# One core, a gated mix of an H3 convolution and dilated local attention: the kernel written anew with an explicit issue order

## The chip, the core and the metric

The program runs on one core of a Trainium2 chip. The core has five engines, each with its own stream of instructions: TensorE (PE: matmuls from SBUF into PSUM; a matmul loads its stationary operand first, shown as PEld), VectorE (DVE), ScalarE (ACT), GpSimd (POOL) and SyncE (SP, which here only issues DMAs; POOL issues others). The metric is the device time of one execution in microseconds, lower is better. The median of three runs of the kernel before is 402.83 us (400.19 to 403.54).

## What is computed

```python
def _A_ref(q, k, v, shift_k, ssm_k, ssm_D):          # S = 2048, D = 640, 4 taps
    k_shift = sum of k shifted by 0..3 rows, times shift_k
    kv = k_shift * v
    y = causal convolution of kv with ssm_k along S  # rfft of length 4096, product, irfft
    return q * (y + kv * ssm_D)
def _B_ref(x, wqkv, wo):                             # 32 heads of 20; window of 8 keys, step 2
    q, k, v = split(x @ wqkv)
    logits = q . k[pos - 2*w], w = 0..7, masked where pos - 2*w < 0
    return (softmax(logits) @ v[pos - 2*w]) @ wo
x = A_q
g = sigmoid((x * gate_w).sum(-1))
return g * a + (1 - g) * b                           # a = _A_ref(x, ...), b = _B_ref(x, ...)
```

(shortened to the formulas). All tensors are 2,048 x 640 in bf16, wqkv is 640 x 1,920.

## The kernel before

Three functions run one after the other; the order of instructions inside them is chosen by the framework's planner, which ranks ready instructions by priority and estimated cost. Only the matmuls of the transform are held in program order by a token (L191).

*b_proj* (L330) loads x, transposes it with PE into xT, and computes q and k feature-major (L376: 128 features x 512 positions from five matmuls, copied to stg by ACT, L379). Each head's 20 features are then moved by SP's DMAs from stg into q32 and k32, where a head begins on a multiple of 32 partitions (L388). The values are projected in 18 blocks of 114 positions (L404, L406), with a column of ones per head in VW that later gives the softmax sum. Beside it, DVE forms kv (*a_kv*, L93): four quarters, each with four products and three additions of 2,560 elements per partition (L131 to L134) and a product with v that also reorders (L135). POOL's queue loads k and v for it (L116, L121, L124).

*b_attn* (L409) walks over block groups outside and eight groups of four heads inside: 40 steps of up to four blocks. A step has scores for two pairs of heads (L454), exp by ACT (L460), a product with the band mask by DVE (L461), PV matmuls with the masked exps as stationary operand (L476), a reciprocal and a product by DVE (L481, L485). After eight steps the group's output is transposed (L495), multiplied with wo (L423), scaled with 1 - g (L426) and written to the DRAM scratch b_scr by SP.

*a_fft* (L149) computes the convolution as a transform of 32 x 64 points in two steps, for four groups of 20 channels in each of eight slots. Per group: first step for the filter (h) and for kv (u) (s1, L206, evacuated to Am by ACT, L196); second step in 64-row halves of the array (s2, L224, L226), evacuated for h by DVE together with the addition of D (L244), for u by ACT (L261); a copy of Hs with its halves swapped (L247, L248); two products (L263, L264); the inverse's first step (L278, evacuated to Cm by ACT) and its second (L298 on), whose result DVE multiplies with g * A_q (L307) and POOL, in the last group DVE, adds b to (L308). The output leaves with the last group (L315). The tables Gre, Gim, Hre, Him, A_q and b_scr are loaded at the start of this function (L167 to L183), into memory that attention has used.

## Time and profile before

| | |
|---|---|
| median of three runs | 402.83 us (400.19 to 403.54) |
| span of the profiled execution, first to last instruction | 400.5 us |
| busy: PE, PEld, DVE, ACT, POOL | 274.8, 183.9, 229.0, 194.6, 91.8 us |
| DMA | 37.37 MB in 26,552 packets, mean 93 GB/s |
| granted TensorE clock, mean over the span | 0.777 |

The profile gives no other time for that execution than its span, which lies inside the range of the runs. A row of a group of instructions reads: line, engine, operation, output and input tile, shape, count, then busy time and the mean of one instruction in ns, then the time its engine idled before them and what ended that idle time. Busy PE time is modelled, since matmuls overlap in the array; a PE that is busy need not be at its peak.

### The profile page before, as it was taken

What the parts mean: (1) busy time and instruction counts of PE and PEld (TensorE: products, weight loads), DVE (VectorE), ACT (ScalarE), POOL (GpSimd) and SP (SyncE); (2) the same over time, 40 slices, a digit from 0 to 9 for tenths busy, and PEclk for the clock granted to TensorE, in tenths of its full rate; (3) what the DMA queues carried; (4) which work ended last, traced back from release to release, by engine and by line L of the source; (5) the groups of instructions that cost most, each with busy time, mean ns of one, the idle gap of its engine ahead of it and who ended that gap; (6) DMA issues with size and microseconds to landing.
All of it is one profiled execution on the core that took longest, in us unless ns stands there. A gap on an engine that the chain in (4) does not pass through costs nothing. (4 is left out here: it accounts for less than half of the span.)

```text
span 400.5 us, 9049 instructions
## 1 busy us (share of the span) xinstructions
PE 274.8 (69%) x3958; PEld 183.9 (46%) x3958; DVE 229.0 (57%) x294; ACT 194.6 (49%) x302; POOL 91.8 (23%) x97
## 2 busy tenths in 40 slices
PE   0699999875543697978878676861766784787640
PEld 0465555332222465555545345641653573476630
DVE  0331094999698867666685307649753538083540
ACT  1025545422543758585875282860446391936310
POOL 5029502090005300000000061000046008102840
PEclk9999999989655568685859596785696697769695
DMA  8926997575334901010101079999000000000047
GB/s 235 283 75 108 163 183 172 111 156 63 68 112 90 173 19 36 18 52 2 51 2 50 34 259 275 231 291 138 0 3 2 2 2 2 2 2 4 2 95 169
DMA packets 26552, 37.37 MB, mean 93 GB/s; under 512 B 15616, under 2 KB 21364, under 8 KB 26000
## 3 DMA queue, kind: packets, MB, share of 16 engines
q1 hardware_dynamic: 21136, 19.62, 20.8%
q0 software_dynamic: 5232, 17.13, 19.7%
q8 instruction: 31, 0.51, 0.6%
q14 instruction: 9, 0.07, 0.1%
q10 hardware_dynamic: 144, 0.04, 0.0%
HBM read 26.26 MB, written 5.25 MB: 79 GB/s over the span
## 5 line engine op out<-in xcount | busy, mean ns | idle before, releaser
L460 ACT ACTIVATE ET<-sc 128x912 bf16<-128x912 f32 (+1 forms) x80 | 63.9, 855 | 21.2 <-PE O L476 11.0
L376 PE MATMUL pj<-xT,W 128*128 128x512 bf16 x200 | 49.9, 405 | 10.0 <-ACT stg L379 10.0
L308 POOL TENSOR_TENSOR a_lin<-a_lin,b_lin 128x480 bf16<-128x480 bf16 (+1 forms) x18 | 32.8, 1856 | 104.1 <-DVE a_lin L307 104.1
L461 DVE TENSOR_TENSOR ET<-ET,band 128x912 bf16<-128x912 bf16 (+1 forms) x80 | 45.4, 570 | 14.5 <-ACT ET L460 13.3
L190 PE MATMUL pb<-Am,Gre 64*128 64x80 bf16 x512 | 32.4, 233 | 27.4 <-DVE Hs L244 14.7
L196 ACT CAST Am<-pa 128x512 bf16<-128x512 f32 x80 | 41.2, 725 | 17.4 <-PE pa L190 17.4
L454 PE MATMUL sc<-q,k 20*128 20x114 bf16 x576 | 32.0, 257 | 18.8 <-ACT ET L460 17.7
L190 PEld LDWEIGHTS <-Gim 64*128 64x128 bf16 x512 | 27.9, 119 | 31.7 <-issue 31.7
L196 ACT CAST Cm<-pa 128x512 bf16<-128x512 f32 x40 | 21.0, 612 | 42.7 <-PE pa L190 42.7
L244 DVE TENSOR_TENSOR Hs<-pb,Dg 128x960 bf16<-128x960 f32 (+1 forms) x24 | 23.9, 1041 | 29.5 <-PE pb L190 29.4
L379 ACT CAST stg<-pj 128x512 bf16<-128x512 f32 x40 | 22.6, 589 | 30.8 <-PE pj L376 20.1
L376 PEld LDWEIGHTS <-W 128*128 128x128 bf16 x200 | 20.3, 103 | 35.5 <-issue 16.0
L423 PE MATMUL op<-wo,oT 128*128 128x512 bf16 (+1 forms) x160 | 33.1, 362 | 3.4 <-ACT fin L426 3.4
L190 PE MATMUL pb<-Am,Gim 64*128 64x80 bf16 x512 | 33.1, 235 | 0.0
L476 PE MATMUL O<-VW,ET 128*128 128x21 bf16 x576 | 22.4, 179 | 13.1 <-DVE o_S L485 12.8
L406 ACT CAST VW<-psv 128x640 bf16<-128x640 f32 x18 | 12.6, 700 | 36.5 <-PE psv L404 36.5
L307 DVE TENSOR_TENSOR a_lin<-pa,a_lin 128x480 bf16<-128x480 f32 (+1 forms) x24 | 13.3, 591 | 28.9 <-PE pa L190 28.9
L190 PEld LDWEIGHTS <-Gre 64*128 64x128 bf16 x512 | 28.7, 119 | 1.1 <-issue 0.8
L476 PEld LDWEIGHTS <-ET 128*128 128x128 bf16 x576 | 19.3, 102 | 18.3 <-issue 12.7
L454 PEld LDWEIGHTS <-k 20*128 20x128 bf16 x576 | 16.7, 107 | 23.2 <-issue 17.9
L190 PE MATMUL pa<-MU,Up 128*128 128x128 bf16 x160 | 24.0, 252 | 3.3 <-DVE a_lin L307 3.3
L426 ACT ACTIVATE fin<-op,omg 128x640 bf16<-128x640 f32 x16 | 12.7, 794 | 27.7 <-PE op L423 19.7
(76 smaller groups left out, 502.8 us busy)
## 6 DMA issues: line engine op xcount, KB each, us to landing
h_lin<-in_A_v_dram POOLq DMA_DIRECT2D x4, 640.0 KB, 16.2
h_lin<-in_A_ssm_k_dram POOLq DMA_DIRECT2D x8, 320.0 KB, 6.7
b_scr<-fin SPq DMA_DIRECT2D x16, 160.0 KB
W<-in_B_wqkv_dram SPq DMA_DIRECT2D x3, 800.0 KB
kh<-in_A_k_dram POOLq DMA_DIRECT2D x12, 190.0 KB, 13.1
q<-stg SPq DMA_DIRECT2D x28, 80.0 KB
k<-stg SPq DMA_DIRECT2D x28, 80.0 KB
Him<-ca_Him POOLq DMA_DIRECT2D x1, 2048.0 KB, 17.7
```

The lines of the kernel that those rows point to most:

```text
L190: inst = nc.tensor.matmul(*args, **kwargs)
L196: nc.scalar.copy(dst, src)
L244: nc.vector.tensor_tensor(Hs[:, :, :, j0:j0 + nj, :], view, Dgv.unsqueeze(3).to_broadcast([128, 2, IL, nj, 4]), ALU.add)
L307: nc.vector.tensor_tensor(reg, yv, reg, ALU.mult)
L308: (nc.vector if g == NG - 1 else nc.gpsimd).tensor_tensor(reg, reg, breg, ALU.add)
L376: nc.tensor.matmul(ps[:], lhsT=W[:, dt, which, 128 * ft:128 * ft + 128], rhs=xT[:, dt, HALO + 512 * sc:HALO + 512 * sc + 512], start=(dt = ...
L379: nc.scalar.copy(stg[:, 512 * sc:512 * sc + 512], ps[:])
L423: nc.tensor.matmul(op[:, n0:n1], lhsT=oT[:, ft, HALO + 128 * sb:HALO + 128 * sb + 128], rhs=wo[:, ft, n0:n1], start=(ft == 0), stop=(ft == ...
L454: nc.tensor.matmul(sc[:, hh, bb * BP:bb * BP + BP], lhsT=k32[32 * h4:32 * h4 + DH, t, kc:kc + 128], rhs=q32[32 * h4:32 * h4 + DH, t, qc:qc ...
L460: nc.scalar.activation(dst, src, ACT.Exp, scale=SCALE)
L461: nc.vector.tensor_tensor(dst, dst, band[:].unsqueeze(1).unsqueeze(1).to_broadcast([128, 2, nbb, BP]), ALU.mult)
L476: nc.tensor.matmul(O[:, slot * 21:slot * 21 + 21], lhsT=ET[:, h4, bb, :], rhs=VW[:, b, h, :], start=True, stop=True, skip_group_check=True)
```

## The change

Everything between the constants and the launch is rewritten. The planner is switched off (`tc.manual_schedule()`): every engine and every queue takes its instructions in the order of the program text, and pieces of work are interleaved by Python generators.

- Positions are split into even and odd ones, so that the window of 8 keys with step 2 becomes 8 neighbours; 17 blocks of 121 queries replace 18 of 114.
- kv is formed in 24 pieces between the value projections, in half quarters; loads of k and v go through SP.
- The band mask leaves DVE: 11 constant rows beside the 20 features of each head in k and q (mk, mq) add 0 inside the window and a large negative number outside, inside the score matmul.
- Attention walks over head groups outside and block groups inside, in 80 half steps. The projection of q and k for the first 256 features (20 of 50 chunks) stands before it, the other 30 chunks stand between half steps 10 and 50. Three buffers of k and q each hold one head group.
- g * A_q is computed early and kept in the DRAM scratch qg_scr. The output projection moves behind attention and runs between the steps of the transform; POOL's queue writes b_scr.
- The transform has five groups of 16 channels per slot; the first step also uses the array's halves, evacuations are 1,024 elements wide and are shared by ACT and DVE by an estimate in the text; the swap Hw is two DMAs, D is added to the filter's first point; the inverse's second step runs once, behind everything, for all channels (160 columns), and the output leaves from there.

The core of the new text (the replaced functions are shown above; memory set-up and constants are cut):

```diff
+BP = 121
+NB = 17
+PRE = 7
+HS = 1024 + PRE
+XW = 2072
+NF = 11
+NT = 8
+KW = 128 * NB
+QW = BP * NB
+GROUPS = [[0, 1, 2, 3], [4, 5, 6, 7], [8, 9, 10], [11, 12, 13], [14, 15, 16]]
...
+NG = 5
+IL = 16
...
+    def pick(self, n):
+        ca, cd = n * 0.833 + 80, n * 1.042 + 70
+        if self.t["a"] + ca <= self.t["d"] + cd:
+            self.t["a"] += ca
+            return "a"
+        self.t["d"] += cd
+        return "d"
...
+    kv = p0.tile([128, 2, 64, 80], BF, name="kv", tag="kv")
+    vl = p0.tile([128, 64, 160], BF, name="vl", tag="hl")
+    xS = p0.tile([128, 16, D], BF, name="xS", tag="oS")
...
+    load_x(0); load_w(2); load_x(1)
...
+    load_kv(0)
+    load_x(2); load_x(3); load_w(0); load_w(1)
+    load_kv(1)
...
+        for h4 in range(4):
+            nc.sync.dma_start(ksets[e][32 * h4 + DH:32 * h4 + DH + NF, :], ca["mk"].ap())
+            nc.sync.dma_start(qsets[e][32 * h4 + DH:32 * h4 + DH + NF, :], ca["mq"].ap())
...
+    def kv_gen():
...
+        for c in range(4):
+            kh = khs[c]
+            for hf in range(2):
+                n0 = 8 * hf
+                pr = p1.tile([128, 4, 8, 160], BF, name="pr", tag="pr")
+                for j in range(4):
+                    nc.vector.tensor_tensor(pr[:, j], kh[:, n0 + 3 - j:n0 + 11 - j, :],
+                                            wl[:, j, :].unsqueeze(1).to_broadcast([128, 8, 160]), ALU.mult)
+                    if j % 2 == 1:
+                        yield
+                nc.vector.tensor_tensor(pr[:, 0:2], pr[:, 0:2], pr[:, 2:4], ALU.add)
+                nc.vector.tensor_tensor(pr[:, 0], pr[:, 0], pr[:, 1], ALU.add)
+                n = 16 * c + n0
+                nc.vector.tensor_tensor(kv[:, :, n:n + 8, :].rearrange("p c n i -> p n c i"),
+                                        pr[:, 0].rearrange("p n (c i) -> p n c i", c=2),
+                                        vl[:, n:n + 8, :].rearrange("p n (c i) -> p n c i", c=2), ALU.mult)
+                yield
+            if c < 2:
+                load_kv(c + 2)
...
+    kvg = kv_gen()
...
+    def qk_gen(engs):
+        for ft in range(NDT):
+            for which in range(2):
+                stg = p1.tile([128, KW], BF, name="stg", tag="stg", bufs=2)
...
+                        yield
+                f0 = 128 * ft
+                for h in range(f0 // DH, (f0 + 127) // DH + 1):
+                    fa, fb = max(DH * h, f0), min(DH * h + DH, f0 + 128)
+                    r = 32 * (h % 4) + fa - DH * h
+                    dst = (qsets if which == 0 else ksets)[(h // 4) % 3]
+                    w = QW if which == 0 else KW
+                    frag = (dst[r:r + fb - fa, 0:w], stg[fa - f0:fb - f0, 0:w])
+                    if h // 4 - 3 < done_t[0]:
+                        nc.sync.dma_start(*frag)
+                    else:
+                        pending.append((h // 4, frag))
...
+    for c in range(3):
+        transposes(c)
+        for b in range(4 * c, 4 * c + 4):
+            vproj(b)
+            advance(kvg, 1)
+    transposes(3)
+    gate()
+    for sb in range(16):
+        nc.vector.tensor_scalar(xS[:, sb, :], xS[:, sb, :], g_sb[:, sb:sb + 1], None, ALU.mult)
+    for c in range(4):
+        nc.sync.dma_start(qg_scr.rearrange("(t p two) d -> p two t d", p=128, two=2)[:, c // 2, 4 * (c % 2):4 * (c % 2) + 4, :],
+                            xS[:, 4 * c:4 * c + 4, :])
...
+    def scores_done(t):
+        done_t[0] = t + 1
+        for fr in [p for p in pending if p[0] - 3 == t]:
+            nc.sync.dma_start(*fr[1])
...
+    qk = qk_gen(lambda ft, w, c: "a" if ft < 2 else "d")
+    advance(qk, 10)
+    advance(kvg, 4)
+    for b in range(12, NB):
+        vproj(b)
+        advance(kvg, 1)
+    advance(qk, 10)
...
+    def scores(s):
+        t, gi, hf = halves[s]
+        blocks = GROUPS[gi]
+        nw = BP * len(blocks)
+        kb, qb = ksets[t % 3], qsets[t % 3]
+        sc = ppa.tile([128, 2, 512], F32, name="sc", tag="sc")
+        for bb, b in enumerate(blocks):
+            for hh in range(2):
+                r = 32 * (2 * hf + hh)
+                nc.tensor.matmul(sc[:, hh, BP * bb:BP * bb + BP], lhsT=kb[r:r + DH + NF, 128 * b:128 * b + 128],
+                                 rhs=qb[r:r + DH + NF, BP * b:BP * b + BP], start=True, stop=True,
+                                 tile_position=(r, 0), skip_group_check=True)
+        nc.scalar.activation(ETs[s % NET][:, :, 0:nw], sc[:, :, 0:nw], ACT.Exp, scale=SCALE)
...
+    scores(0)
+    for s in range(len(halves)):
+        if s + 1 < len(halves):
+            scores(s + 1)
+            if s + 1 == len(halves) - 1 or halves[s + 2][0] != halves[s + 1][0]:
+                scores_done(halves[s + 1][0])
+        if 10 <= s < 20 or 21 <= s < 31 or 41 <= s < 51:
+            advance(qk, 1)
+        advance(kvg, 1)
+        pv(s)
...
+    for q in range(4):
+        for c in range(2):
+            base = A_ssm_k[160 * q + 80 * c:160 * q + 80 * c + 80, :]
+            src = bass.AP(tensor=base.tensor, offset=base.offset, ap=[[64, 32], [S, 80], [1, 64]])
+            nc.sync.dma_start(h_lin[32 * q:32 * q + 32, :, c, :], src)
...
+    p2 = ctx.enter_context(tc.tile_pool(name="p2", bufs=1, reuse_waits="tile"))
...
+    G = p2.tile([128, 32, 2, 128], BF, name="G")
+    nc.sync.dma_start(G[:], cf["G"].ap().rearrange("p (a r b) -> p a r b", a=32, r=2))
...
+    def op_gen():
+        for b in range(NB):
+            tr = pp2.tile([128, NDT, 128], BF, name="tr", tag="ps")
+            for ft in range(NDT):
+                nc.tensor.transpose(tr[:, ft, 0:BP], oS[0:BP, b, 128 * ft:128 * ft + 128], ident[0:BP, 0:BP])
+            oT = oTs[b % 3]
+            ld.copy(oT[:, :, 0:BP], tr[:, :, 0:BP], 605)
+            yield
...
+            if ld.pick(640) == "a":
+                nc.scalar.activation(fin[0:BP, :], opf[0:BP, 0:D], ACT.Copy, scale=omg[0:BP, b:b + 1])
+            else:
+                nc.vector.tensor_scalar(fin[0:BP, :], opf[0:BP, 0:D], omg[0:BP, b:b + 1], None, ALU.mult)
+            for r0, n, dst in pos_rows(b_scr, BP * b, BP):
+                nc.gpsimd.dma_start(dst, fin[r0:r0 + n, :])
+            yield
...
+    def s1_gen(key, X, g):
+        Am = p2.tile([128, 64, 4, IL], BF, name="Am", tag="Am", bufs=3)
+        st[key] = Am
+        for oc in range(2):
...
+            for il in range(8):
+                i = IL * g + 8 * oc + il
+                for qp in range(2):
+                    rows = slice(64 * qp, 64 * qp + 64)
+                    if key[0] == "h":
+                        lhsT = X[rows, i, :, :].rearrange("p c n -> p (c n)")
+                    else:
+                        lhsT = X[rows, :, :, i].rearrange("p c n -> p (c n)")
+                    o = pss[qp][:, il // 4, 128 * (il % 4):128 * (il % 4) + 128]
+                    nc.tensor.matmul(o, lhsT=lhsT, rhs=F1b[rows, :], start=True, stop=True,
+                                     tile_position=(64 * qp, 0), skip_group_check=True)
+            for qp in range(2):
+                src = pss[qp][:].rearrange("p a (l q j) -> p j q (a l)", l=4, q=2)
+                ld.copy(Am[:, :, 2 * qp:2 * qp + 2, 8 * oc:8 * oc + 8], src, 1024)
...
+    def s2_gen(key, dst):
+        Am = st.pop(key)
+        for jb in range(4):
+            ps = ps_tile("s2")
+            for jj in range(8):
+                j = 8 * jb + jj
+                for r in range(2):
+                    for c in range(2):
+                        rows = slice(64 * c, 64 * c + 64)
+                        nc.tensor.matmul(ps[:, c, 64 * jj:64 * jj + 64], lhsT=G[rows, j, r, :],
+                                         rhs=Am[rows, 2 * j + r, :, :].rearrange("p q l -> p (q l)"),
+                                         start=(r == 0), stop=(r == 1), tile_position=(64 * c, 0), skip_group_check=True)
+            ld.copy(dst[:, :, 8 * jb:8 * jb + 8, :, :].rearrange("p c j q l -> p c (j q l)"), ps[:], 1024)
...
+    def h_s2(g):
+        Hs = p2.tile([128, 2, 32, 4, IL], BF, name="Hs", tag="Hs", bufs=2)
+        yield from s2_gen(("h", g), Hs)
+        Hw = p2.tile([128, 2, 32, 4, IL], BF, name="Hw", tag="Hw")
+        nc.sync.dma_start(Hw[0:64], Hs[64:128])
+        nc.sync.dma_start(Hw[64:128], Hs[0:64])
...
+    def u_s2(g):
+        Up = p2.tile([128, 2, 32, 4, IL], BF, name="Up", tag="Up", bufs=2)
+        yield from s2_gen(("u", g), Up)
+        Hs, Hw = st.pop(("H", g))
+        Vp = p2.tile([128, 2, 32, 4, IL], BF, name="Vp", tag="Vp")
+        for c in range(2):
+            nc.vector.tensor_tensor(Vp[:, c], Up[:, c], Hw[:, c], ALU.mult)
+            nc.vector.tensor_tensor(Up[:, c], Up[:, c], Hs[:, c], ALU.mult)
+        ld.t["d"] += 4500
+        st[("UV", g)] = (Up, Vp)
...
+    def inv1(g):
+        Up, Vp = st.pop(("UV", g))
...
+                ps = ps_tile("i1")
+                for il in range(8):
+                    o = ps[:, il // 4, 128 * (il % 4):128 * (il % 4) + 128]
+                    for k, src in ((0, Up), (1, Vp)):
+                        nc.tensor.matmul(o, lhsT=src[:, c, :, :, 8 * oc + il].rearrange("p j q -> p (j q)"), rhs=M[:, k, :],
+                                         start=(k == 0), stop=(k == 1), skip_group_check=True)
+                i0 = IL * g + 8 * oc
+                ld.copy(Cm[:, :, :, c, i0:i0 + 8].rearrange("p n r l -> p (n r) l"),
+                        ps[:].rearrange("p a (l m) -> p m (a l)", l=4), 1024)
...
+    def fft_gen():
+        yield from s1_gen(("h", 0), h_lin, 0)
+        yield from h_s2(0)
+        yield from s1_gen(("u", 0), kv, 0)
+        for g in range(NG):
+            if g + 1 < NG:
+                yield from s1_gen(("h", g + 1), h_lin, g + 1)
+            yield from u_s2(g)
+            if g + 1 < NG:
+                yield from h_s2(g + 1)
+                yield from s1_gen(("u", g + 1), kv, g + 1)
+            yield from inv1(g)
+    fft = fft_gen(); opg = op_gen()
+    k = 0
+    while advance(fft, 1):
+        k += 1
+        if k >= 2:
+            advance(opg, 1)
+    while advance(opg, 1):
+        pass
...
+    qg = p0.tile([128, 64, 160], BF, name="qg", tag="hl")
+    bl = p0.tile([128, 64, 160], BF, name="bl", tag="kv")
+    tabs = []
+    for k in range(4):
+        tb = p2.tile([128, 2, 16, 128], BF, name="tab", tag="Am" if k < 3 else "Hw", bufs=3 if k < 3 else 1)
+        nc.sync.dma_start(tb[:], cf["T"].ap()[:, 4096 * k:4096 * k + 4096].rearrange("p (r a b) -> p r a b", r=2, a=16))
+        tabs.append(tb)
+    for q in range(4):
+        nc.sync.dma_start(qg[32 * q:32 * q + 32], lin_src(qg_scr, q, 0, 64))
+    for q in range(4):
+        nc.gpsimd.dma_start(bl[32 * q:32 * q + 32], lin_src(b_scr, q, 0, 64))
+    for n0 in range(0, 64, 6):
...
+        ps = ps_tile("i2")
+        for k in range(nn):
+            n2 = n0 + k
+            o = ps[:, k // 3, 160 * (k % 3):160 * (k % 3) + 160]
+            for r in range(2):
+                nc.tensor.matmul(o, lhsT=tabs[n2 // 16][:, r, n2 % 16, :], rhs=Cm[:, n2, r, :, :].rearrange("p c i -> p (c i)"),
+                                 start=(r == 0), stop=(r == 1), skip_group_check=True)
+        for hb in range(0, nn, 3):
+            m = min(3, nn - hb)
+            reg = qg[:, n0 + hb:n0 + hb + m, :]
+            yv = ps[:, hb // 3, 0:160 * m].rearrange("p (n c) -> p n c", n=m)
+            nc.vector.tensor_tensor(reg, yv, reg, ALU.mult)
+        reg = qg[:, n0:n0 + nn, :]
+        nc.vector.tensor_tensor(reg, reg, bl[:, n0:n0 + nn, :], ALU.add)
+        for q in range(4):
+            dst = outf[:, 160 * q:160 * q + 160].rearrange("(a b) c -> a b c", b=64)[:, n0:n0 + nn, :]
+            (nc.sync, nc.gpsimd)[q % 2].dma_start(dst, reg[32 * q:32 * q + 32])
```

722 lines of the change are left out of this document (261 added, 461 removed).

## The prediction

> **What bounds the kernel now.** The chain of waits ends after a few links (its shares add up to a few per cent), so it names no bound. I cut the span at the places where the kind of work changes and read the busy time in each stretch.
>
> ```profile
> core 0: us, PE busy (x) PEld busy (x) DVE busy (x) ACT busy (x) POOL busy (x), PEclk, DMA share, GB/s
> 0.00:13.00 13.00, 0.88 (x8) 0.72 (x9) 0.00 (x0) 1.28 (x1) 5.64 (x13) 1.00 0.86 267
> 13.00:108.00 95.00, 81.47 (x551) 41.92 (x550) 58.22 (x38) 36.97 (x61) 31.71 (x41) 0.95 0.68 132
> 108.00:235.00 127.00, 91.00 (x1400) 59.03 (x1400) 85.75 (x184) 77.45 (x102) 12.27 (x13) 0.66 0.23 57
> 235.00:283.00 48.00, 27.09 (x443) 19.39 (x442) 30.71 (x16) 23.29 (x43) 4.70 (x6) 0.68 0.98 236
> 283.00:388.00 105.00, 74.35 (x1560) 62.88 (x1559) 54.29 (x57) 55.59 (x98) 35.09 (x22) 0.80 0.03 6
> 388.00:400.50 12.50, 0.00 (x0) 0.00 (x0) 0.00 (x0) 0.00 (x0) 2.37 (x4) 0.55 0.79 177
> ```
>
> Loading takes 13 us. The projections (95 us) are held by PE. Attention with its output projection (127 us) fills no engine: PE 72%, DVE 68%, ACT 61%. The first 48 us of the transform run at the rate of the DMA (share 0.98), which brings tables, A_q and b_scr only then. The next 105 us again fill nothing, with ACT and DVE at half. The last 12.5 us only write out. So 232 us of 400 are stretches in which the engines wait for each other:
>
> ```profile
> POOL a_lin L308 <- DVE a_lin L307: 104.1, 3, 54.4
> ACT Cm L196 <- PE pa L190: 42.7, 14, 17.8
> DVE Hs L244 <- PE pb L190: 29.4, 4, 10.9
> PE sc L454 <- ACT ET L460: 17.7, 27, 2.4
> PE pb L190 <- DVE Hs L244: 14.7, 11, 10.8
> ```
>
> PE waits for DVE and DVE for PE. The first row is POOL's idle time and costs nothing.
>
> **The prices.** Groups of instructions, shapes apart (busy time, then mean of one):
>
> ```profile
> L460 ACT ACTIVATE ET<-sc 128x912 bf16<-128x912 f32 x64 | 55.9, 931 | 20.1 <-PE O L476 10.6 <-PE sc L454 9.4
> L461 DVE TENSOR_TENSOR ET<-ET,band 128x912 bf16<-128x912 bf16 x64 | 39.4, 616 | 13.1 <-ACT ET L460 12.0
> L196 ACT CAST Cm<-pa 128x512 bf16<-128x512 f32 x40 | 21.0, 612 | 42.7 <-PE pa L190 42.7
> L244 DVE TENSOR_TENSOR Hs<-pb,Dg 128x960 bf16<-128x960 f32 x20 | 22.3, 1153 | 29.5 <-PE pb L190 29.4
> L261 ACT CAST Up<-pb 128x960 bf16<-128x960 f32 x20 | 18.1, 1021 | 8.6 <-issue 8.2 <-PE pb L190 0.4
> L135 DVE TENSOR_TENSOR kv<-acc,h_lin 128x2560 bf16<-128x2560 bf16 x4 | 18.0, 4504 | 3.4 <-DMA kh<-in_A_k_dram 3.4
> L133 DVE TENSOR_TENSOR tmp<-kh,wl 128x2560 bf16<-128x2560 bf16 x12 | 17.9, 1488 | 0.2
> L307 DVE TENSOR_TENSOR a_lin<-pa,a_lin 128x480 bf16<-128x480 f32 x20 | 12.4, 648 | 28.9 <-PE pa L190 28.9
> L264 DVE TENSOR_TENSOR Up<-Up,Hs 128x5120 bf16<-128x5120 bf16 x4 | 12.3, 3082 | 0.0
> L247 DVE COPY Hsw<-Hs 64x5120 bf16<-64x5120 bf16 x4 | 6.0, 1489 | 0.1
> L308 DVE TENSOR_TENSOR a_lin<-a_lin,b_lin 128x480 bf16<-128x480 bf16 x5 | 1.8, 398 | 0.0
> L315 POOL DMA_DIRECT2D out_dram<-a_lin x7 | 4.6, 668 | 7.2 <-issue 7.0 <-DVE a_lin L307 0.3
> ```
>
> Rates, from runs of equal instructions in the timeline (start, length, engine, count) and from short stretches whose columns are as above:
>
> ```profile
> 27.76 8.79 PE L376 MATMUL pj<-xT,W 128*128 128x512 bf16 x40
> 101.26 4.43 PE L376 MATMUL pj<-xT,W 128*128 128x512 bf16 x10 [5.29 <-ACT stg L379]
> 152.51 3.39 ACT L460 ACTIVATE ET<-sc 128x912 bf16<-128x912 f32 x4
> 154.31 0.38 PE L454 MATMUL sc<-q,k 20*128 20x114 bf16 x8 [0.36 <-ACT ET L460]
> 155.38 0.56 PE L476 MATMUL O<-VW,ET 128*128 128x21 bf16 x16
> 170.47 1.53 PE L423 MATMUL op<-wo,oT 128*128 128x512 bf16 x10
> 285.10:286.20 1.10, 1.10 (x13) 1.10 (x12) 1.09 (x2) 0.73 (x2) 0.00 (x0) 0.50 0.00 0
> 379.50:380.50 1.00, 1.00 (x22) 1.00 (x20) 0.00 (x0) 1.00 (x4) 0.00 (x0) 1.00 0.00 0
> 269.10:269.90 0.80, 0.73 (x24) 0.73 (x24) 0.80 (x2) 0.00 (x0) 0.00 (x0) 0.50 1.00 430
> 349.50:350.50 1.00, 0.91 (x48) 0.91 (x48) 0.26 (x1) 0.04 (x1) 0.00 (x0) 1.00 0.00 0
> 100.00:104.00 4.00, 2.74 (x7) 1.01 (x7) 3.97 (x2) 1.48 (x3) 0.00 (x0) 0.50 0.46 103
> 273.00:276.00 3.00, 0.00 (x0) 0.00 (x0) 3.00 (x1) 0.00 (x0) 0.00 (x0) 0.50 1.30 194
> 4.00:8.00 4.00, 0.00 (x0) 0.10 (x1) 0.00 (x0) 0.00 (x0) 2.68 (x4) 1.00 1.08 356
> ```
>
> So a 512-column matmul costs 220 ns at clock 1.00 and 443 at 0.50; a 128-column one of the inverse step about 55 and 107 (1.00 us over 22 less those still draining, and 1.10 over 13 likewise); one on a 64-row half of the array, 80 columns, 19 and 30; a score matmul 47, a PV one 35; an output projection of one block 1.53 us. Loads move 356 GB/s in rows of 1,280 bytes, 194 GB/s in runs of 320 bytes on SP's queue alone (b_lin, 273 to 276 us), and head fragments about 103 GB/s.
>
> **Stage 1, up to the first scores: 80 us.** PE needs 17 value blocks x 1.4 (five times 220 and five of a quarter), 20 of the 50 q/k chunks x 1.1 (four are short), 80 transposes and the gate: about 52 us. DVE has the longer list. kv is now 32 products, 8 wide adds, 8 short adds and 8 products with v: at L133's price for 2,560 elements, and half for 1,280, 8 x 6 = 48 us, 14 less than now, since kv is laid out so that L135's 4,504 ns fall to half of L133's rate. 21 of its 24 pieces are queued before attention: 42 us, and with its copies of xT and the scaling of A_q by g (14,300 elements at the same 0.58 ns) 50. It cannot begin before the first quarter of k and v: SP sends x, W_v, x (2.1 MB at 356 = 6 us) and then 1.43 MB of 320-byte runs at 194 (7.4 us): 16 us with the start. DVE's copy of the second group of xT stands behind the kv pieces, so PE waits for that DMA too. And SP is now a single file: masks, k and v, the write of qg (waits for DVE), the fragments of q and k (1.1 MB per 128 features, 11 us at 103) stand before the last quarter of k and v. When DVE has scaled A_q, qg (2.6 MB, 7 us), one set of fragments (11) and that quarter (7.4) are still to move, 25 us, and DVE has six pieces, some 11 us, to do meanwhile: I add 14 us, 16 + 50 + 14 = 80; without such waits 66.
>
> **Attention: 88 us.** The 64 band products leave DVE and leave the loop exp, product, PV. 80 exps remain: a burst costs 848 ns per 912 elements, so in proportion 0.90 us for four blocks of 121 (32 exps) and 0.68 for three (48): 61 us, as before. sc, O and ET have two, two and six buffers, so the loop may run at ACT's pace: the 50 halves without a projection chunk cost 50 x 0.77, and 10% for the round trip, 42 us. In the other 30 PE carries 24 whole chunks (1.1) and six short ones (0.28), 28 us, beside 13.6 score and PV matmuls per half (0.56 us): 30 x 0.56 + 28 = 45 us, PE-bound, 73 at half clock. The projections now ran at clock 0.95, so I take 46. The chunks' evacuation by DVE hides beside them, as DVE has lost L461's 39 us; the mask rows widen the contraction from 20 to 31 of the 32 rows and the same columns pass.
>
> **Transform with the output projection: 100 us.** Evacuation: 40 tiles of the first step, 40 of the second and 20 of the inverse, 1,024 elements each, 1.08 us as the mean of both engines (busy time over count, 0.91 us of ACT in L261 and 1.12 of DVE in L244 for 960): 108 us; 17 blocks of transposed output and projection, 1,245 elements each, 22; DVE's 20 products of 2,048 elements at L264's 0.6 ns, 24. Together 154, shared by two engines: 77. PE: 320 half-array matmuls of 128 columns at 28 ns (an estimate: two at once, half of 55), 1,280 of 64 columns at 15 to 19, 320 at 55, and 17 x (1.53 + 0.3): about 80 us at clock 1.00, 145 at 0.50. Gone are the Hsw copies (12 us with L248, now two DMAs with a whole group of slack) and the add of D (now one small add to h_lin). G and h_lin load during the second half of attention, under PE and ACT, not in a 48 us block; without that cover h_lin alone, 2.6 MB, would cost at least 14 us at 194 GB/s. The writes of b_scr move from SP to POOL, which has nothing else to do. Two loads near 80 under one fixed order and four PSUM tiles will not overlap fully: I take 92 (an estimate, 77 to 100 are its ends), and 8 for the last group, whose products nothing covers: 100.
>
> **Tail: 40 us.** All of the last step is now last. DVE: 22 x 0.62 (L307) + 11 x 0.72 (two L308) = 21 us; PE's 128 matmuls hide. Before it stands a wait: SP issues the four parts of the last table and then qg; the fourth part goes into Hw's place and waits for the last group's products, about 4 us before the transform ends. Behind it 1 MB (3 us) and qg's 2.62 MB in 320-byte runs (13.5 us): qg lands 13 us after the transform. b_scr is read back earlier, on POOL's queue. The output keeps up, also in POOL's issues (two of 0.67 us per tile of 1.9; SP has the other two): 0.25 MB per 1.9 us is 129 GB/s, below the 177 of the last 12.5 us. 5 us for the last to land: 13 + 1 + 21 + 5 = 40; 27 if qg is in time.
>
> Sum: 80 + 88 + 100 + 40 = 308 us against the span of 400.5. That span is 2.3 us under the median of the runs (402.83), which I add: **310**.
>
> **A cost that no row shows.** The 480 stationary operands of kv, Up and Vp are now read with a step (160 or 32 bytes); all of now are contiguous. Bounds: nothing (a 128-column pair stays at 55 ns), or the DVE case, where L135's stepped operand took three times L133's time: 480 x 2 x 55 = 53 us on PE. I take nothing, the nearest row being a weight load, and keep 53 us of PE work, of which cover would hide about 20, for the range. The Trainium skill (TensorE: Matmul & The Clock Gate, "Weight-path perf modes") allows steps from -1,023 to 1,024 elements for the fast weight load, which gives the sum as it stands; no run here shows it.
>
> **Rivals.** *Better overlap* (0.14): stage 1 66, attention 85, transform 90, tail 27 = 268, 270 with the offset. For it: every piece has slack somewhere; against: SP's single file. *Clock* (0.15): PE stays at half clock wherever it waits often. Attention 88 + 20, transform 125 (about midway between 100 and PE's 145): 80 + 108 + 125 + 40 = 353, 355. For it: 0.66 and 0.80 in the stages of short matmuls; against: PE would be denser. The Trainium skill (the same page, "A second HAM failure mode: psum-queue depth-cycling") says that micro-idles between groups that cycle through PSUM throttle the clock; the stages at 0.66 to 0.80 agree, and by that rule the time would be this rival's. *Stepped weights* (0.04), the other side: if each of the 480 loads cost 250 ns more on PE's path, 120 us would come on top of 310: 430; it decides from 195 ns, 94 us. *Not what it says* (0.05): G and h_lin are not early, because places in memory come free late: 14 us, 324. The forecast itself has 0.62, 285 to 330.
>
> The range 272 to 348 holds the forecast, the late loads, half of the overlap case (258 to 284) and a third of the clock case (335 to 372): 0.62 + 0.05 + 0.07 + 0.05, about 0.8. A difference below about 1% cannot be told from no change (the runs lie between 400.19 and 403.54). Faster 0.95, same 0.01, slower 0.04.
>
> **What would show it.** First scores near 80 us, with DVE, not PE, the fuller engine before; exps in bursts at 0.7 to 0.9 us and 1.7 where chunks run; in the transform ACT and DVE above 75%; a DVE wait of about 13 us for qg behind the last Cm. I am wrong if qg is there in time, if the clock falls below 0.8 in attention or transform, if the short half-array matmuls of the stepped loads exceed 60 ns, or if stage 1 ends before 68 or after 92.

## The result and the profile after

The changed kernel takes **357.2 us** (median of 4 runs, 354.5 to 360.4) against 402.4 us: ratio **0.886**, 95% interval 0.882 to 0.891. The forecast was 310 us, range 272 to 348: the direction held, the time lies outside. All ratios below are to the kernel before on the same chip and, like the intervals, come from undisturbed runs, while the stage lengths of each kernel come from one profiled execution, which in bl_early and filler ran about 1% longer than the median and in tail_early, s1_order and best2 about 1% shorter. The profiled execution of the changed kernel has a span of 354.9 us. Cut at the first scores, the last exp and the last evacuated Cm (columns as in the prediction):

```profile
core 0: us, PE busy (x) PEld busy (x) DVE busy (x) ACT busy (x) POOL busy (x), PEclk, DMA share, GB/s
0.00:90.50 90.50, 61.37 (x434) 33.36 (x438) 55.47 (x70) 28.63 (x46) 24.13 (x41) 0.83 0.91 189
90.50:187.50 97.00, 84.62 (x1233) 52.26 (x1232) 51.56 (x118) 67.13 (x82) 0.00 (x0) 0.75 0.42 86
187.50:302.10 114.60, 96.06 (x2181) 76.86 (x2182) 75.76 (x74) 76.66 (x84) 13.87 (x22) 0.91 0.43 108
302.10:354.90 52.80, 12.95 (x128) 10.83 (x127) 19.29 (x33) 0.00 (x0) 12.50 (x22) 0.64 0.76 161
```

| stage | forecast | measured | over |
|---|---|---|---|
| to the first scores | 80 | 90.5 | 10.5 |
| attention | 88 | 97.0 | 9.0 |
| transform and projection | 100 | 114.6 | 14.6 |
| tail | 40 | 52.8 | 12.8 |

The 47 us are spread over all four. In stage 1 no engine is full but the DMA share is 0.91; in the transform PE is busy 84%, DVE and ACT 66 and 67%: PE is the fullest there, not the engines that evacuate (*contig*, below, tests it). Rows of the waits (us in total, times, longest):

```profile
DVE qg L613 <- DMA qg<-qg_scr: 33.6, 1, 33.6
POOL bl L599 <- PE s L510: 28.8, 1, 28.8
PE psv L308 <- DVE xT L130: 12.7, 2, 9.6
ACT stg L128 <- DMA kb<-stg: 6.9, 1, 6.9
PE O L424 <- DVE oS L432: 4.2, 2, 2.4
```

The first two belong to the tail: POOL holds the read of bl until PE has read kv for the last time, and DVE waits for qg. The next two are stage 1: PE behind DVE's kv pieces, and ACT (with PE behind it) for a stg buffer whose fragments have not gone out. The last is PE behind kv pieces in the first halves. Groups of instructions, shapes apart, as in the prediction:

```profile
L410 ACT ACTIVATE ET<-sc 128x726 bf16<-128x726 f32 x48 | 36.5, 779 | 19.3 <-PE sc L407 19.1
L410 ACT ACTIVATE ET<-sc 128x968 bf16<-128x968 f32 x32 | 30.5, 976 | 10.6 <-PE sc L407 10.2
L130 DVE CAST Am<-s 128x1024 bf16<-128x1024 f32 x19 | 22.9, 1221 | 7.0 <-PE s L510 6.8
L128 ACT CAST Am<-s 128x1024 bf16<-128x1024 f32 x21 | 21.2, 1021 | 6.1 <-PE s L510 6.0
L510 PEld LDWEIGHTS <-kv 64*128 64x128 bf16 x160 | 7.5, 178 | 2.3 <-issue 1.7
L510 PEld LDWEIGHTS <-h_lin 64*128 64x128 bf16 x160 | 5.5, 103 | 5.0 <-issue 2.5 <-DVE h_lin L458 1.8
L559 PEld LDWEIGHTS <-Up 128*128 128x128 bf16 x160 | 21.9, 153 | 4.1 <-issue 3.8
```

Evacuations cost 1.02 us (ACT) and 1.22 us (DVE), near the 1.08 forecast as a mean. The stepped loads (kv, Up) are the slow ones.

### The profile page after: what moved, and what is told of

It is laid out like the page before. It is cut to its first block, busy times and chain, and to the rows that moved or that the text cites. A ratio compares the mean times of both kernels' runs of the same rounds, so it can differ in the third digit from the quotient of the medians.

```text
span 354.9 us, 9099 instructions
## 1 busy us (share of the span) xinstructions
PE 255.0 (72%) x3971; PEld 173.3 (49%) x3971; DVE 202.1 (57%) x294; ACT 172.4 (49%) x211; POOL 50.5 (14%) x85
## 5 line engine op out<-in xcount | busy, mean ns | idle before, releaser
L410 ACT ACTIVATE ET<-sc 128x726 bf16<-128x726 f32 (+1 forms) x80 | 66.7, 858 | 29.9 <-PE sc L407 29.3
L341 PE MATMUL pj<-xT,W 128*128 128x484 bf16 (+3 forms) x250 | 58.3, 379 | 6.9 <-ACT stg L128 6.9
L308 PE MATMUL psv<-W,xT 128*128 128x128 bf16 (+1 forms) x170 | 31.6, 357 | 12.7 <-DVE xT L130 12.7
L341 PEld LDWEIGHTS <-W 128*128 128x128 bf16 x250 | 22.1, 104 | 32.3 <-issue 15.7
L274 DVE TENSOR_TENSOR pr<-kh,wl 128x1280 bf16<-128x1280 bf16 x32 | 24.3, 819 | 21.6 <-DMA kh<-in_A_k_dram 12.1
L407 PE MATMUL sc<-qb,kb 31*128 31x121 bf16 x544 | 34.9, 255 | 0.0
L613 DVE TENSOR_TENSOR qg<-i,qg 128x480 bf16<-128x480 f32 (+1 forms) x22 | 13.0, 635 | 33.6 <-DMA qg<-qg_scr 33.6
L483 PE MATMUL op<-wo,oT 128*128 128x128 bf16 (+1 forms) x170 | 27.3, 310 | 3.8 <-ACT oT L128 2.8
L559 PE MATMUL i<-M,Up 128*128 128x128 bf16 x160 | 24.6, 248 | 4.3 <-DVE Up L547 3.8
L526 PE MATMUL s<-Am,G 64*128 64x64 bf16 x1280 | 24.7, 192 | 3.9 <-issue 2.5
L130 DVE CAST Am<-s 128x1024 bf16<-128x1024 f32 x19 | 22.9, 1221 | 7.0 <-PE s L510 6.8
L526 PEld LDWEIGHTS <-G 64*128 64x128 bf16 x1280 | 21.3, 96 | 7.0 <-issue 5.0
L559 PE MATMUL i<-M,Vp 128*128 128x128 bf16 x160 | 24.5, 247 | 0.0
```

The source lines that it names most:

```text
L130: self.nc.vector.tensor_copy(dst, src)
L274: nc.vector.tensor_tensor(pr[:, j], kh[:, n0 + 3 - j:n0 + 11 - j, :], wl[:, j, :].unsqueeze(1).to_broadcast([128, 8, 160]), ALU.mult)
L308: nc.tensor.matmul(ps[:, n0:n1], lhsT=xT[:, dt, BP * b:BP * b + 128], rhs=W[:, dt, 2, n0:n1], start=(dt == 0), stop=(dt == NDT - 1))
L341: nc.tensor.matmul(ps[:, 0:n], lhsT=W[:, dt, which, 128 * ft:128 * ft + 128], rhs=rhs, start=(dt == 0), stop=(dt == NDT - 1))
L407: nc.tensor.matmul(sc[:, hh, BP * bb:BP * bb + BP], lhsT=kb[r:r + DH + NF, 128 * b:128 * b + 128], rhs=qb[r:r + DH + NF, BP * b:BP * b + B ...
L410: nc.scalar.activation(ETs[s % NET][:, :, 0:nw], sc[:, :, 0:nw], ACT.Exp, scale=SCALE)
```

## Experiments

| run | us | ratio, interval | first scores | attention | transform | tail |
|---|---|---|---|---|---|---|
| changed kernel | 357.2 | 0.886 (0.882-0.891) | 90.5 | 97.0 | 114.6 | 52.8 |
| tail_swap | 346.9 | 0.863 (0.857-0.868) | 89.1 | 97.1 | 114.5 | 45.0 |
| tail_early | 342.2 | 0.843 (0.836-0.851) | 89.0 | 97.4 | 125.1 | 25.0 |
| bl_early | 341.2 | 0.848 (0.842-0.854) | 93.6 | 97.8 | 118.6 | 34.7 |
| op_first | 347.9 | 0.865 (0.859-0.870) | 89.1 | 97.2 | 125.4 | 33.8 |
| contig | 356.8 | 0.886 (0.879-0.893) | 92.4 | 97.6 | 111.4 | 55.9 |
| act_xt | 357.7 | 0.888 (0.883-0.893) | 91.6 | 97.1 | 114.7 | 52.5 |
| s1_pool | 370.1 | 0.918 (0.912-0.923) | 99.7 | 100.0 | 114.6 | 53.8 |
| s1_dma | 370.2 | 0.919 (0.913-0.925) | 92.7 | 107.3 | 114.3 | 52.9 |
| s1_qg | 357.7 | 0.890 (0.883-0.898) | 82.3 | 105.3 | 114.6 | 53.2 |
| s1_order | 346.4 | 0.858 (0.850-0.867) | 71.4 | 102.3 | 113.9 | 52.6 |
| both | 329.7 | 0.820 (0.815-0.826) | 71.5 | 104.7 | 118.2 | 33.8 |
| best | 330.3 | 0.822 (0.819-0.826) | 68.2 | 111.6 | 119.4 | 29.8 |
| best2 | 333.7 | 0.822 (0.815-0.830) | 70.9 | 108.8 | 118.3 | 29.3 |
| best3 | 332.8 | 0.825 (0.820-0.829) | 70.5 | 109.8 | 124.3 | 25.5 |
| best4 | **321.8** | **0.801** (0.797-0.806) | 70.7 | 99.8 | 119.1 | 29.9 |
| filler | 357.2 | 0.886 (0.880-0.891) | 94.1 | 97.2 | 114.9 | 53.3 |
| no_kv4 | 352.9 | one run | 89.7 | 92.9 | 114.9 | 53.6 |
| band_back | 374.5 | one run | 90.2 | 115.0 | 114.8 | 52.7 |

**The tail.** *tail_swap* puts qg's four loads ahead of the tables on SP; *tail_early* asks for both early, on POOL:

```diff
+ bl = p0.tile(..., name="bl", tag="oS")      # behind the last op_gen step
+ st["qg"] = p0.tile(..., name="qg", tag="hl") # in fft_gen, behind s1 of h(4)
+ nc.gpsimd.dma_start(...)                    # both, four parts each
```

> Only SP's order is changed: qg is asked for ahead of the four tables. Theory A (late by place, 9.2 MB behind two late slots): qg starts at 283.7 instead of 295.9 us and the tables follow it; the bytes stay the same, and DVE can begin when qg and the first table are in, with three tables still under way: 6 to 10 us less, 347 to 351 us. Theory C (the order on SP alone is the fault, as the prediction's sum had it): 12 us or more, 345 us or less. Theory B (the last byte sets the end): 357 us, no difference.

> Theory A (the last step's inputs are asked for too late: bl behind the last kv product at 283.7 us, qg behind the last table at 295.9 us, so that 9.2 MB move in 283.7 to 331 while the engines wait): with bl in oS's place, asked for as soon as the output projection is done (about 255 us), and qg asked for as soon as h_lin is dead (about 274 us), both on POOL's queue, both are there when the transform ends; the tail falls from 52.8 us to about 28 (1 + 18.7 of DVE + 5, and a few for the last table), 332 to 336 us in all. Theory B (the bytes set the end, and loads beside the transform hold up its products' evacuation or the exchange of Hs): the transform grows by what the tail loses, no better than 348 us.

The changed kernel's SP asks for the tables and qg only here (start, length of issue; the second row shows the first two of qg's four parts):

```profile
283.67 12.23 SPq L594 DMA_DIRECT2D tab<-cf_T  x4
295.95 20.87 SPq L597 DMA_DIRECT2D qg<-qg_scr  x2
```

Swapping gave 10 us, as theory A said (346.9 against 347 to 351); in tail_swap's waits PE then stands for the tables:

```profile
PE i L607 <- DMA tab<-cf_T: 19.9, 1, 19.9
```

With both early the tail was 25 us, below the 28 of theory A, but the transform grew by 10.5 us. Theory A holds for the tail; of its gain a good third was lost again, so the total lies between the two theories. The loss is not where the next expectation puts it, on the exchange of Hs. PE's wait at L526, the second step, in the changed kernel and in tail_early, then two rows of tail_early's timeline:

```profile
PE s L526 <- issue: 2.5, 2, 1.4
PE s L526 <- issue: 11.4, 3, 4.9
281.93 3.47 PE L526 MATMUL s<-Am,G 64*128 64x64 bf16 x128 [2.97 <-issue]
283.50 1.23 DVE L546 TENSOR_TENSOR Vp<-Up,Hw 128x2048 bf16<-128x2048 bf16 x1 [3.96 <-ACT Up L128]
```

DVE's wait ended with ACT's copy of Up, which stood behind PE, and PE waited for nothing that the profile shows ("issue"). The trace has one more thing at these places: packets of 16 KB on the DMA queue q8, of the kind "instruction" (31 of them in the changed kernel, 0.51 MB). In the 19 runs from the changed kernel on, PE stood 27 times for over 1.2 us at the second step by "issue", and each time it went on 1.3 to 1.7 us after such a packet had ended. In tail_early the longer stalls (3.0 to 4.9 us) lie where the 320-byte loads keep the DMA share at 0.9 to 1.04. So it looks as if PE waited for its own instructions, which came late beside these loads; that is read from the times, no run tests it. The next kernel, *bl_early*, was made on the exchange's account: bl as above, qg on SP behind the last exchange.

> bl goes into oS's place as soon as the projection is done (POOL's queue, about 255 us); qg stands on SP ahead of the tables, behind the last exchange of Hs, not beside it. Theory N (tail_early lost 9 us because 320-byte loads of bl and qg delayed two exchanges of Hs by some 10 us; one load alone is over before it matters): transform 112 to 117 us, then 6.6 MB from 283 to about 312 us, DVE's first product at 302 to 308: 329 to 335 us in all. Theory B (any load beside the transform costs what it saves): 342 us or more, as tail_early.

The transform grew by some 4 us (118.2 in *both*, below, against 113.9 in s1_order, which differ by this edit; PE's stalls by "issue" at the second step are 7.0 and 2.4 us), and qg and the tables behind the last exchange held the end again: 341 us, no better than tail_early. Theory N fails.

**The transform.** *op_first* takes the projection out of it (bl and qg placed as in bl_early).

> The output projection stands whole ahead of the transform, its transposes one block ahead of its products; bl goes into oS's place right behind it (POOL's queue), qg ahead of the tables on SP behind the last exchange of Hs. Theory P (PE's work bounds the transform, 95.7 us busy of 114.2, and loads beside the exchange of Hs are what cost tail_early its gain): transform with projection 110 to 116 us, tail about 28 to 32 us: 328 to 338 us. Theory Q (the projection covered the transform's waits, as the prediction had it): the transform alone runs at the pace of its last two groups, 15 us each, behind some 36 us of projection: 120 us or more, 340 us or more.

The transform with projection grew by 10.8 us and the total is 347.9 us, both inside theory Q's bounds, but the waits do not show theory Q's cause:

```profile
PE s L525 <- issue: 13.7, 5, 5.3
```

bl is read beside the second steps here too, and this stall (L525 is the second step in op_first) is 11.2 us longer than in the changed kernel. Without it the two transforms take 111.7 and 112.1 us (tail_early 113.7, bl_early 111.2, both 111.2). What the interleaving is worth on its own is not shown. *contig* makes the stepped operands contiguous:

```diff
- lhsT = X[rows, :, :, i].rearrange("p c n -> p (c n)")
+ lhsT = X[rows].rearrange("p c n i -> p (c n i)")[:, 128 * i:128 * i + 128]
```

> The stepped stationary operands of the first step of kv and of the inverse are replaced by contiguous slices of the same tiles (same sizes and counts, so the transform's result is not the reference's). Theory S (steps cost: 54 against 38 ns for a kv matmul and 65 against 55 for an inverse one): 160 x 16 + 320 x 10 ns = 5.8 us of PE less, in a stage where PE is busy 84%: 352 to 355 us. Theory T (the step is free, the rest is clock and buffers): within 1 us of 357.

From 200 to 283 us the loads of kv fell from 178 to 94 ns and those of Up from 149 to 105 (contig's groups in that stretch, then its transform):

```profile
L510 PEld LDWEIGHTS <-kv 64*128 64x128 bf16 x146 | 4.5, 94 | 2.4 <-issue 1.8
L559 PEld LDWEIGHTS <-Up 128*128 128x128 bf16 x96 | 10.0, 105 | 0.3 <-issue 0.2
190.00:301.40 111.40, 91.95 (x2181) 71.36 (x2182) 75.68 (x74) 75.79 (x85) 13.83 (x22) 0.92 0.41 102
```

PE lost 4.1 us of work and the transform 3.2. The total did not move, as theory T had it: the tail took 3.1 back, since its loads were asked for no earlier (bl at 284.7 us, 283.7 in the changed kernel). So the step costs PE time, as theory S had it, but not at the end.

**Stage 1.** Five kernels: *act_xt* copies all of xT on ACT (`eng="a"`); *s1_pool* moves masks and qg's write to POOL's queue; *s1_dma* puts two thirds of the masks and the last quarter of k and v behind the first scores; *s1_qg* moves only qg's write, *s1_order* combines it with act_xt and sorts the masks:

```diff
-    for c in range(4): nc.sync.dma_start(qg_scr..., xS...)
     advance(qk, 10)                 # fragments of the first 128 features
+    for c in range(4): nc.sync.dma_start(qg_scr..., xS...)
```

> All copies of xT go to ACT, none to DVE. PE no longer waits 10 us (18.6 to 28.7 us) behind DVE's kv pieces. Theory E (this wait is what makes stage 1 late): first scores 7 to 10 us earlier, 347 to 350 us in all. Theory D (SP's single file sets it): the value projections come earlier, but the fragments and the last quarter of k and v do not, as SP still has masks and the third quarter until 57 us: 0 to 3 us, 354 to 357 us.

> The 24 mask loads and the four writes of qg leave SP's queue for POOL's. Theory D (stage 1 is late by SP's single file): the third quarter of k and v starts about 10 us earlier, the fragments no longer stand behind 2.6 MB of qg, and the first scores come at 78 to 82 us instead of 90.5: 345 to 349 us in all. Theory E (DVE's own list and its copy of xT in the middle of it hold stage 1): first scores within 3 us of 90.5, 354 us or more.

> 16 of the 24 mask loads (0.75 MB, head groups 1 and 2) are asked for after the last projection ahead of attention, and the last quarter of k and v (1.4 MB) in the middle of attention, with its six kv pieces; SP keeps all else. Theory F (the DMA engines' own time bounds stage 1; their share is 1.07, 0.96, 0.86 and 1.03 between 20 and 90 us): 2.1 MB less in it, about 14 us at the paces of the rows (103 and 194 GB/s), first scores at 76 to 82 us; the two stalls of PE in the first halves (5.7 us) go as well: 338 to 346 us in all. Theory E (the lists of PE and DVE hold stage 1): first scores within 4 us of 90.5, only the stalls go: 350 to 354 us.

In act_xt q's projection began at 37.8 us instead of 54.7, and nothing was gained, as theory D said; its waits:

```profile
ACT stg L128 <- DMA qb<-stg: 24.7, 1, 24.7
PE pj L341 <- ACT stg L128: 24.6, 3, 24.0
```

PE stood until 82.0 us for fragments that stood behind masks, k and v and qg's write. But emptying SP's file (s1_pool) made it worse: the masks then ran beside the first k and v, whose first products came at 25.2 us instead of 20.2. The first scores came at 99.7 us, outside the bounds of both theories. And 2.1 MB less in the stage (s1_dma) brought nothing there (92.7 us) and 10 us more in attention, so that theory F fails and the total is also above theory E's. What is left is the order, which the next two kernels change.

> One thing moved: the four writes of qg on SP stand behind the fragments of the first 128 features, not ahead of them. Theory H (these fragments, 11.2 us of issue for q behind 2.6 MB of qg, hold the two stg buffers, and PE's wait for them, 74.7 to 80.9 us, is on the path): no wait for stg, first scores at 83 to 86 us, 350 to 353 us in all. Theory M (the last quarter of k and v now comes later still, and DVE gives the gain back in the first halves): first scores early, but 355 to 359 us in all.

> All copies of xT on ACT (which alone gave nothing, as PE then waited 24 us for the fragments), and SP's order changed: masks of head group 0, third quarter of k and v, fragments of the first 128 features, last quarter, masks of group 1, qg's write, fragments of the second 128, masks of group 2. Theory H (stage 1 is PE's chain plus the order of SP's transfers): first scores at 66 to 76 us and part of it given back in the first 20 halves, 338 to 346 us in all. Theory M (DVE's kv list, 42 us from 20 us on, is the next bound): first halves stall until DVE is through at about 90 us, 348 to 355 us in all.

s1_qg took 8 us off stage 1, as theory H said, and gave all back in attention, as M said; a row of its waits:

```profile
DVE pr L274 <- DMA qb<-stg: 14.7, 1, 14.7
```

(the row names the last semaphore; it is the last quarter of k, sent later, that the product reads). In s1_order stage 1 fell by 19 us, as theory H said, and attention grew by 5; its 346.4 us lie just above H's bounds.

**Order followed to its end.** *both* is s1_order with bl_early. In *best* qg's write comes directly behind the first fragments, kv pieces are single operations, and qg comes in two parts between the tables; *best2* sends the second fragments before the last quarter of k and v; *best3* is best2 with qg asked for on SP between two exchanges of Hs; *best4* is best2 with:

```diff
-    load_kv(3)
-    load_masks(2)                   # behind the second fragments
...
+        if s == 9: load_masks(2); load_kv(3)   # behind scores_done(0)
-        if s >= 12: advance(kvg, 1)
+        if s >= 14: advance(kvg, 1)
```

> s1_order and bl_early together. The stages follow one another, so the gains add: by theories H and N 312 to 326 us, by M and B 335 to 350 us.

> Made from the kernel with both orders: qg's write stands directly behind the fragments of the first 128 features (in that kernel the first write into oS, which takes xS's place, waited 9.5 us for it), kv pieces are cut into single operations and those of the last quarter begin at the fifth half, qg comes in two parts between the tables (table, half of qg, table, half of qg, two tables), and POOL clears ET and oT behind its loads. Theory H+N (the order of transfers, not their number, sets these stages): first scores at 70 to 75 us, attention 94 to 98 us instead of 104.7, DVE's first product of the tail within 3 us of the last Cm: 311 to 320 us in all. Theory M (DVE now waits for the last quarter and returns the gain): 321 to 328 us. The copy of wl took 6.79 us beside these clears: under 1 us if they slowed it, 5 to 7 us if not.

> Made from best, in which the first halves no longer stalled but PE waited 16 us at the halves of head group 1 for its masks and fragments (landed at 81 and 98 us behind qg's write and the last quarter of k and v). Here the order on SP is: fragments of the first 128 features, qg's write, masks of group 1, fragments of the second 128, last quarter of k and v, masks of group 2; kv pieces of that quarter begin at the thirteenth half. Theory H (order alone): first scores at 66 to 72 us, attention 93 to 98 us instead of 111.6: 312 to 318 us in all. Theory M (the wait moves on to DVE or to head group 2): attention 103 us or more, 322 to 330 us.

> Made from best2, in which PE waited 10 us (DVE 16 us for a stg buffer) because the last two fragments of the second 128 features, for head group 3, stood on SP behind the last quarter of k and v and the masks of group 2. Now both come behind these fragments, in the tenth half, and the kv pieces begin at the fifteenth. Theory H (order alone): attention 93 to 99 us instead of 108.8 in best2, 312 to 321 us in all. Theory M (the wait moves on once more): attention 103 us or more, 325 to 333 us.

Stage 1 and the tail kept their gains, and each time the wait turned up inside attention: on oS (9.5 us, both), on the masks and fragments of head group 1 (best), on stg for the fragments of head group 3 (best2). Both's 329.7 us lie between its two pairs of theories. Best and best2 stood where both stood, and their totals are even 2 and 4 us above theory M's bounds. Best3 was expected 4 to 8 us under best2, or, if qg held up the last exchange, no better with a transform 6 us or more longer; the second came: 332.8 us, transform 124.3 instead of 118.3 us, of which PE's stalls by "issue" are 2.2 and DVE's wait for that exchange 1.9. In best4 attention is 2.8 us longer than in the changed kernel (a DVE wait of 6.1 us for fragments is left) and the total 321.8 us, less than in any other kernel here and just above theory H's bounds (99 and 321 us). Its stages:

```profile
0.00:70.70 70.70, 56.49 (x432) 32.00 (x434) 43.22 (x61) 32.06 (x50) 23.97 (x41) 0.90 0.87 196
70.70:170.50 99.80, 85.07 (x1233) 52.41 (x1232) 53.46 (x122) 67.32 (x82) 0.00 (x0) 0.78 0.60 120
170.50:289.60 119.10, 96.42 (x2181) 76.84 (x2182) 75.87 (x74) 76.89 (x84) 13.87 (x22) 0.91 0.52 117
289.60:319.50 29.90, 11.23 (x128) 10.63 (x127) 19.37 (x33) 0.00 (x0) 12.49 (x22) 0.79 0.88 219
```

PE, DVE and ACT have nearly the work that they have in the changed kernel (249, 192 and 176 us busy against 255, 202 and 172); most of the 35 us by which it is faster than the changed kernel are waits.

**Attention.** *no_kv4* leaves out three kv pieces, *filler* adds a 128-column product per plain half, *band_back* adds `tensor_tensor(et, et, et, ALU.max)` behind each exp.

> The last eighth of kv (the three DVE pieces that stand in the first halves of attention) is left out and that eighth is zero. Theory U (these pieces, which PE waits for twice, are most of attention's 9.4 us over the forecast): attention 91 to 93 us instead of 97.4. Theory K (half clock is most of it): 95 to 97 us.

> In the 50 halves without a projection chunk PE does one more 128-column product into unused columns of the O tile, while it waits for exp. Theory K (PE's short waits lower its clock; clock 0.75, 0.84 and 0.68 in the three thirds of attention, half until 10 us into the transform): the clock stays near 1.00, attention falls by about 5 us and the transform's start by as much: 347 to 353 us. Theory L (the clock does not follow these waits): 50 x 55 to 110 ns more, 357 to 362 us.

> The mask stays in the scores, but a DVE product over every ET tile comes back between exp and PV (maximum of ET with itself, which changes nothing), as the band product stood before. By 616 ns per 912 elements 80 of them are 44 us of DVE. Theory W (its place in the chain exp, product, PV is what the mask saves): each plain half longer by about 0.65 us, chunk halves by less: attention longer by 25 to 45 us, 382 to 402 us in all. Theory X (six ET buffers hide it): attention longer by less than 10 us, 357 to 367 us.

Attention of no_kv4 and of band_back, in the columns above:

```profile
89.70:182.60 92.90, 84.24 (x1234) 51.85 (x1232) 46.74 (x113) 67.26 (x82) 0.00 (x0) 0.78 0.46 95
90.20:205.20 115.00, 85.67 (x1234) 52.85 (x1232) 93.17 (x200) 67.72 (x82) 0.00 (x0) 0.72 0.38 80
```

No_kv4 (first row): the three pieces were 4.1 of the 9.0 us, theory U. Filler: the time is the same, as theory L had it; the clock of its attention was 0.77 instead of the 1.00 that theory K expected, so this run does not tell what the clock costs. Band_back (second row): 41.6 us more of DVE made attention 18 us longer, between W and X. A product of this size between exp and PV, where the band product stood, would take back 18 of the 45 us that the change gained. No_kv4 and band_back ran once each; the kernels that leave attention alone have 97.0 to 97.8 us there, so both differences stand out.

## Why the forecast was wrong, point by point

- **Stage 1, 80 us.** The lists of PE and DVE were of the right size (61 us with the slow clock, 55). PE, not DVE, was the fuller engine. The step that failed is "I add 14 us": SP's transfers were added up behind DVE's list, on which they were believed to wait. The wait was on PE's chain, projection, stg, fragments, stg, with qg's write between. With SP's order changed and the copies of xT on ACT, s1_order reached 71.4 us.
- **Attention, 88 us.** Left out was that DVE's kv pieces stand before the evacuation of O (4.1 us, shown). Without them the plain halves took 44.4 us, forecast 42, and the chunk halves 48.0, forecast 46. Three times ten chunk halves of the same make-up, from first exp to first exp:

```profile
103.60:120.20 16.60, 16.60 (x184) 9.15 (x181) 8.47 (x19) 8.46 (x10) 0.00 (x0) 0.84 0.14 29
121.10:135.70 14.60, 14.45 (x184) 8.60 (x185) 8.24 (x18) 8.55 (x11) 0.00 (x0) 1.00 0.33 70
144.50:161.30 16.80, 16.77 (x185) 9.42 (x186) 8.08 (x18) 8.62 (x11) 0.00 (x0) 0.84 0.20 42
```

  PE is full in all three, as forecast, and a half takes 1.46 us at clock 1.00 and about 1.67 at 0.84: 4.2 us of attention go with the clock here, where 0.95 was taken from stage 1 of before. The plain halves behind the first ten took 0.87 to 0.92 us at clocks from 0.50 to 1.00. No run sets the clock, so its share is read, not tested.
- **Transform, 100 us.** The step that failed is PE's term: "about 80 us at clock 1.00" was mis-sized; PE was busy 96, and ACT and DVE came to 67 and 66%, not above 75. The changed kernel's timeline (start, length) at full clock:

```profile
201.59 0.88 PE L510 MATMUL s<-F1b,kv 64*128 64x128 bf16 x16
202.41 1.53 PE L483 MATMUL op<-wo,oT 128*128 128x512 bf16 x10
203.88 0.85 PE L510 MATMUL s<-F1b,kv 64*128 64x128 bf16 x16
...
207.90 0.62 PE L510 MATMUL s<-F1b,h_lin 64*128 64x128 bf16 x16
208.45 0.44 PE L475 MATMUL tr<-ident,oS 121*128 121x121 bf16 x5
...
211.79 0.64 PE L526 MATMUL s<-Am,G 64*128 64x64 bf16 x32
212.36 0.44 PE L475 MATMUL tr<-ident,oS 121*128 121x121 bf16 x5
212.74 0.64 PE L526 MATMUL s<-Am,G 64*128 64x64 bf16 x32
```

  From start to start: kv 0.82/16 = 51 ns, h_lin 34, the second step 17.8, projection 1.47 and transposes 0.38 us; the inverse 62 ns. With the counts 160, 160, 1,280, 17 and 320 that is 88 us, 8 more than forecast, half of it the step that was taken "at nothing". The mean clock of 0.91 makes about 96 of 88. The 18.5 us of waits on top are what the forecast allowed for (20). The Trainium skill (TensorE: Matmul & The Clock Gate, "Weight-path perf modes") allows these steps for the fast weight load. The page gives no price for them; the loads at 178 and 149 ns against 94 and 105 show that an allowed step was not a free one here, and the measurement decides.
- **Tail, 40 us.** DVE (19.7 us from its first product to its last) and the last landing (4.8) held. "b_scr is read back earlier" failed: bl waits for kv's place until 283.7 us, and the tables come no earlier, so that 9.4 MB (four tables, qg and bl), not 3.6, move from there on. DVE's wait for qg was 33.6 us instead of 13.
- **Rivals.** The time is near the clock rival's 355 by luck, not by its way: it had attention at 108 and the transform at 125 us (measured 97.0 and 114.6). Its sign did come in attention (clock 0.75, below 0.8). But in the transform the stretch with the last of the projection ran at full clock:

```profile
230.00:253.20 23.20, 21.60 (x446) 15.20 (x446) 15.09 (x17) 15.92 (x18) 3.73 (x7) 1.00 0.20 57
```

  By the Trainium skill (the same page, "A second HAM failure mode: psum-queue depth-cycling") short idle times between groups that cycle through PSUM make the clock fall and rise. Attention at 0.75 agrees; in this row the groups cycle through four PSUM tiles, PE is busy 93%, and the clock stays at 1.00, so that cycling alone did not lower it. The late loads were not G and h_lin (which came under attention, but for 1.8 us), but bl, tables and qg.

## What to carry to other kernels

Price a queue written in order by walking it: for each transfer ask which buffer it frees and who waits for that buffer, instead of adding its bytes to one engine's list. A wait removed by order turns up at the next buffer, so follow it until the stages add up (here it took four kernels, s1_order, best, best2 and best4). For a load that takes a dead tile's place, look up when the tile dies. And before moving a load beside a stage of many short matmuls, look at what PE waits for at "issue" there.

## What was not expected of the hardware

POOL's clears slow a DVE copy. In the changed kernel it ran beside them (row of its groups), in best they came later (row of its timeline):

```profile
L267 DVE COPY wl<-wraw 128x640 bf16<-128x640 bf16 x1 | 6.8, 6793 | 0.7 <-DMA wraw<-in_A_shift_k_dram 0.7
```

```profile
9.20 0.49 DVE L270 COPY wl<-wraw 128x640 bf16<-128x640 bf16 x1 [9.20 <-DMA wraw<-in_A_shift_k_dram]
```

6.79 us against 0.49. The clears ran from 8.3 to 15.5 us in the changed kernel, and the copy ended at 15.8, 0.3 us behind the last of them; in best they began at 15.7.

Loads beside short matmuls made PE stand by "issue" (11.4 us in tail_early, 2.5 in the changed kernel), each time until just behind a packet of the instruction queue; that it stood for its instructions is read from this, not tested.

What sets the clock in attention stays open: in the changed kernel it was at half between 163 and 187 us although PE was busy 20.6 of these 24 us:

```profile
163.00:187.00 24.00, 20.58 (x354) 13.74 (x354) 9.33 (x27) 21.74 (x28) 0.00 (x0) 0.51 0.97 185
```
